# Weight sums of one batch queued in small groups behind dense adds, their tiles fetched a step ahead, and block sums made later

## The chip, the cores and the metric

The kernel runs on one core of a Trainium2 chip. TensorE multiplies matrices, VectorE (DVE in the profile), ScalarE (ACT) and GpSimd (POOL) work element by element, and SyncE (SP) issues nearly all of the transfers between memory and SBUF. The engines run side by side; each works through its own instructions in the order in which the program puts them. The metric is the device time of one execution in microseconds, lower is better, as the median of several runs.

## The reference

An attention block feeds a block that mixes with a Fourier transform. There are 4 batches, 8 heads, 768 tokens and 64 elements per head, all in fp32. Cut to what matters:

```python
# attention: a window of +-15 tokens, and 24 block summaries per head
k_sum = k.reshape(B, H, nb, 32, D).max(axis=3)
v_sum = v.reshape(B, H, nb, 32, D).mean(axis=3)
scores_l = where(|i - j| < 16, q @ k.T / 8, -1e9)
scores_s = q @ k_sum.T / 8 + log(32)
a = softmax(concat([scores_l, scores_s]))
x = a @ concat([v, v_sum])            # heads side by side: (B, 768, 512)
# mixing
u = x + real(fft(fft(x, axis=1), axis=2))
un = (u - mean(u)) / sqrt(var(u) + 1e-6)
out = u + max(un @ w_ch1, 0) @ w_ch2  # 512 -> 2048 -> 512
```

## The kernel before

The four batches go through a pipeline: while batch b is in its two dense layers, the attention of batch b+1 is worked on beside it.

The two dense layers are made with Strassen's scheme in Winograd's form: seven products of half-size blocks in place of eight. That needs sums of the blocks of both operands. `_left_sums` and `_right_sums` make four such sums each (L477 to L488). The first layer is `gen_hidden(b, c)` (L1278): c is the half of the hidden units, and each half has four steps j of 256 units. One step is seven products (L1293, called hx, hy and hz by the accumulator that they go to), with copies, adds and relus on ScalarE and VectorE in between (L1303 to L1322). A product is 1.29 us of TensorE. The second layer is `gen_out(b, c)` (L1326): three groups of rows, each with four sums of the hidden block on VectorE (s, L1348 to L1351), and seven products of four matmuls (ox, oy, oz, L1358), each added to x by VectorE.

The weights come in as fp64 words and are converted once, during batch 0, by `gen_weights` (L1090) on VectorE and ScalarE; the finished tiles with their sums are stored to DRAM and fetched again by the later batches. An exception are the first four tiles of the second layer: batch 0 stores only their blocks without the sums (L1078 to L1080). In batch 1 `get_w2` (L1112) fetches each of these four (called w, w2_1_0 to w2_1_3), makes the four sums on VectorE at once, and stores them for batches 2 and 3. `gen_hidden` calls `get_w2` for tile j at the head of step j (L1285); the tile's user is `gen_out(1, 0)`, after step 3. The tiles live in four buffers that hold the second half's tiles of the batch before until its last products have read them.

Attention works on four pairs of heads g (`gen_attention`, L960): scores (sc, L776), scores of the block summaries (ss, L792), an exponential on ScalarE and a mask product on VectorE (p with near, L783), then values (`values`, L795): a small product with the block sums (vs, L799), its product with a mask on VectorE (L800), the window's values (av, L809), and the block sums' values (av, L814), which read vs. For the next pair VectorE transposes K and Q (L693) and takes the maximum of each block (km, L717).

The block sums of V themselves (`block_sums`, L604) are made for two pairs at a time, (b, 0) and (b, 1): four loads on SP (vb), and adds that run on VectorE while weights are still being converted, and on GpSimd afterwards (L629 to L639). On GpSimd they use the one large buffer called room, which the Fourier stage also uses. `load_values` calls `block_sums` at odd g for the pairs that come after (L652, L653): block (2, 0) during the attention of batch 1, which runs beside batch 0's dense layers, and (3, 0) during the attention of batch 2. Block (b, 1) of the later batches is made at g = 1 of its own attention (L994).

What sets the order: `drive` (L1422) steps several generators in turn by given rates (in one round, 44 steps of the dense layers and 76 of the attention, L1473), which gives the order in which instructions are recorded; a scheduler then orders them on each engine by its own estimates of when operands are ready, except for the first attention, whose order is fixed by hand. `tc.issue_after(marks["dense"])` keeps an instruction behind the last dense add that was marked. The transfers recorded after batch 0 begins its dense layers may be reordered too (L1469).

Of the kernel before, what the change touches and what calls it, by code (L numbers as in the profile page):

```python
# [483 lines left out]
def _right_sums(tt, b):  # L484
    tt(b(T1), b(B12), b(B11), ALU.subtract)
    tt(b(T2), b(B22), b(T1), ALU.subtract)
    tt(b(T3), b(B22), b(B12), ALU.subtract)
    tt(b(T4), b(B21), b(T2), ALU.subtract)  # L488


def _main_program(ctx, tc, q, k, v, moe_w_ch1, moe_w_ch2, out):
# [3 lines left out]
    B, H, S, D = q.shape  # L495
# [69 lines left out]
    def tt(out, in0, in1, op):  # L565
        return nc.vector.tensor_tensor(out=out, in0=in0, in1=in1, op=op).ins  # L566
# [7 lines left out]
    def load(b, g, *which):  # L574

        for n in which or (1, 0):
            t = nat[b, g, n] = apool.tile([P, 2, NST // 2, 2 * D], FP, tag="nat", bufs=4, name=f"{'qk'[n]}n_{b}_{g}")
            if (b, g) > (2, 0):
                t = nat[b, g, n] = t.rearrange("p e j n -> p (e j n)").rearrange("p (m c) -> p m c", c=32)
                for e in range(2):  # L580
                    for h in range(2):
                        r, o = D * e + 32 * h, (q, k)[n][b, 2 * g + e].offset + 32 * h
                        fetch(out=t[r:r + 32], in_=bass.AP((q, k)[n].tensor, o, [[D, 32], [32 * D, S // 32], [1, 32]]))
                continue
            fetch(out=t.rearrange("p e j n -> p (e j) n"),
                  in_=(q, k)[n][b, 2 * g:2 * g + 2].rearrange("e (j p s) d -> p (e j) (s d)", p=P, s=2))
# [61 lines left out]
    def load_values(b, g):  # L648
        if is_wide(b):
            load_wide_values(b, g)  # L650
            return
        if g % 2 and following(b, g, 1) and (b, g) != (1, 1) and not (b > 1 and g == 1):  # L652
            block_sums(*divmod((b * NP + g + 1) // 2, NP // 2))  # L653
        load_narrow_values(b, g)

    def load_wide_values(b, g):
# [169 lines left out]
    def following(b, g, n):  # L826
        i = b * NP + g + n
        return divmod(i, NP) if i < B * NP else None
# [131 lines left out]
    def gen_attention(b):  # L960
        x = bpool.tile([P, NST, DM], FP, tag="x", bufs=2, name=f"x_{b}")
        x_of[b] = x
        held = None
        if b == 2:
            load(2, 1)
            load(2, 2)
        for g in range(NP + 1):
            n1, n3 = (following(b, g, n) for n in (1, 3))
            if held:
                values(b, g - 1, *held, x)  # L970
                if n1 and b > 1:
                    load_values(*n1)
            if g == NP and b > 1:
                turn_tiles(b, x)
                for _ in range(17):
                    yield
                rooms[b] = room(f"fold_{b}")
                steps = fold_batch(b, split_fold(b, rooms[b]))
                while True:
                    with tc.issue_after(marks["dense"]):  # L980
                        done = next(steps, steps) is steps
                    if done:
                        break
                    yield
            elif held and b > 1:
                yield
                yield
                yield
            if g < NP:
                held = scores(b, g)  # L990
                sum_scores(b, g, held[1])
            if g and n1 and b == 1:
                load_values(*n1)
            if g == 1 and b > 1:  # L994
                block_sums(b, 1)
            if g == NP and b > 1:
                return
            yield
            if g == NP:
                return  # L1000
            if b > 1:
                yield
                yield
            if n1:
                prepare(*n1, *((1,) if b > 1 else ()))
            if b > 1:
                yield
                yield
                if n1:
                    prepare(*n1, 0)  # L1010
            if n3 and not (b == 1 and n3 > (2, 0)):
                load(*n3)
            yield
            if b > 1:
                yield
# [89 lines left out]
    def get_w1(b, j):  # L1105
# [3 lines left out]
        fetch(out=w, in_=dw1[j])  # L1109
        wt[1, b, j] = w  # L1110

    def get_w2(b, j):  # L1112
        w = bpool.tile([P, 7, HD], FP, tag="w2", bufs=NC, name=f"w2_{b}_{j}")
        if b == 0:
            return
        wt[2, b, j] = w
        if b == 1 and j < NC:
            fetch(out=w[:, 0:4], in_=dw2[j][:, 0:4])
            _right_sums(tt, lambda i: w[:, i])
            fetch(out=dw2[j][:, 1:7], in_=w[:, 1:7])  # L1120
        else:
            fetch(out=w, in_=dw2[j])

# [154 lines left out]
    def gen_hidden(b, c):  # L1278
        u = wt["u", b]
        js = range(NC * c, NC * (c + 1))  # L1280
        h = wt["h", b] = bpool.tile([P, NC, 2, S], FP, tag="h", name=f"h_{b}_{c}")
        for j in js:
            if 0 < j < NJ - 2:
                get_w1(b, j + 2)
            get_w2(b, j)  # L1285
            w = wt[1, b, j]
            c11, c12 = h[:, j - NC * c, 0, 0:S2], h[:, j - NC * c, 0, S2:S]
            c21, c22 = h[:, j - NC * c, 1, 0:S2], h[:, j - NC * c, 1, S2:S]
            X, Y, Z = (bank([P, S2], f"h{n}_{b}_{j}") for n in "xyz")

            def product(ps, a, r, start, stop):
                for kk in range(2):
                    ins = nc.tensor.matmul(ps, w[:, a, kk, :], u[:, r, kk, :], start=start and kk == 0,  # L1293
                                           stop=stop and kk == 1, skip_group_check=True)
                marks["hidden", b] = ins.ins

            def relu(t):
                if b:
                    nc.vector.tensor_scalar(out=t, in0=t, scalar1=0.0, scalar2=None, op0=ALU.max)
                else:  # L1300
                    nc.scalar.activation(out=t, in_=t, func=AF.Relu)

            product(X, A11, B11, True, False)  # L1303
            nc.scalar.copy(out=c11, in_=X)  # L1304
            product(Y, A12, B21, True, True)
            marks["dense"] = tt(c11, Y, c11, ADD)
            yield
            product(X, S2_, T2, False, False)
            nc.scalar.copy(out=c12, in_=X)
            product(Z, S1, T1, True, False)  # L1310
            nc.scalar.copy(out=c22, in_=Z)  # L1311
            relu(c11)
            yield
            product(X, S3, T3, False, False)
            marks["dense"] = tt(c22, X, c22, ADD)
            product(Z, S4, B22, False, True)
            marks["dense"] = tt(c12, Z, c12, ADD)
            yield
            product(X, A22, T4, False, True)
            nc.scalar.activation(out=c21, in_=X, func=AF.Relu)  # L1320
            relu(c22)
            relu(c12)  # L1322
            issued.add(("h", b, j))
            yield

    def gen_out(b, c):  # L1326
# [137 lines left out]
    for b in range(B):  # L1464


        most = chain(gen_hidden(b, 0), gen_out(b, 0), gen_hidden(b, 1))
        if b == 0:
            in_order[0] = False  # L1469
            drive((most, 5, 0), (weights, 15, 0), (attn, 1, 0))  # L1470
            done_weights.append(True)
        else:
            drive((most, 44, 0), (gen_attention(b + 1) if b + 1 < B else iter(()), 76, 0))  # L1473
        last = gen_out(b, 1)
        if b + 1 < B:
            drive((gen_fourier(b + 1), 22, 600), (last, 12, 0))
        else:
            drive((last, 1, 0))
        if b == B - 2:

            ok = apool.tile([P, B * NP * 2 * NST], FP, tag="qt", name="ok")
            all_ok = spool.tile([P, 2], FP, tag="all_ok", name="all_ok")
            flag = cpool.tile([1, 1], I32, name="flag")
            rv = rec.rearrange("p n h i -> p (n h i)")
            nc.vector.tensor_scalar(out=ok, in0=rv, scalar1=1.0 / LIM, scalar2=None, op0=ALU.is_ge)
            nc.vector.scalar_tensor_tensor(out=ok, in0=rv, scalar=LIM, in1=ok, op0=ALU.is_le, op1=ALU.mult)
            nc.vector.tensor_reduce(out=all_ok[:, 0:1], in_=ok, op=ALU.min, axis=AX.X)
            nc.vector.memset(all_ok[:, 1:2], 1.0)
            ps = bank([1, 1], "flag_ps")
            nc.tensor.matmul(ps, all_ok[:, 0:1], all_ok[:, 1:2], start=True, stop=True)  # L1490
            nc.vector.tensor_scalar(out=flag, in0=ps, scalar1=P - 0.5, scalar2=None, op0=ALU.is_lt)
# [40 lines left out]
```

## Time and profile before

| | us |
|---|---|
| median of 3 runs | 810.48 |
| lowest and highest | 807.29, 811.65 |
| the profiled execution | 811.17 |
| its span, first to last instruction | 809.3 |
| TensorE matmul busy | 781.9 (97%) |
| TensorE weight load busy, beside it | 571.9 (71%) |
| VectorE busy | 500.8 (62%) |
| ScalarE busy | 224.3 (28%) |
| GpSimd busy | 46.8 (6%) |

The stages, by the span's own clock: the first attention until about 60 us; batch 0's first layer with the weights' conversion and the attention of batch 1, about 92 to 149; its second layer and second half until 287; batch 1's first half from there to 388, and its second half with the Fourier stage of batch 2 until 478; batch 2 likewise until 659; batch 3, with no attention beside it, to the end. A busy TensorE is not TensorE at its peak: its ends are modelled. The name before an arrow is the tile written, behind it the tiles read. The profile's numbers for one product are doubled against the program's: each fp32 matmul shows as two records.

### The profile page before, as it was taken

What the parts mean: (1) busy time and instruction counts of PE and PEld (TensorE: products, weight loads), DVE (VectorE), ACT (ScalarE), POOL (GpSimd) and SP (SyncE); (2) the same over time, 40 slices, a digit from 0 to 9 for tenths busy, and PEclk for the clock granted to TensorE, in tenths of its full rate; (3) what the DMA queues carried; (4) which work ended last, traced back from release to release, by engine and by line L of the source; (5) the groups of instructions that cost most, each with busy time, mean ns of one, the idle gap of its engine ahead of it and who ended that gap; (6) DMA issues with size and microseconds to landing.
All of it is one profiled execution on the core that took longest, in us unless ns stands there. A gap on an engine that the chain in (4) does not pass through costs nothing.

```text
span 809.3 us, 14447 instructions
## 1 busy us (share of the span) xinstructions
PE 781.9 (97%) x5914; PEld 571.9 (71%) x5914; DVE 500.8 (62%) x1135; ACT 224.3 (28%) x493; POOL 46.8 (6%) x85
## 2 busy tenths in 40 slices
PE   8959899999999989999999999999999999999997
PEld 6758665555579856678669876688669875786686
DVE  5778998887998664554476734554476722532352
ACT  3523865543635112200126112200126102001200
POOL 0010000000000220010030300000030000000000
PEclk9979999999999999999999999999999999999999
DMA  9999799769655367939344248511514043205001
GB/s 218 222 198 179 162 320 271 155 224 298 214 165 174 93 202 184 206 86 173 117 176 153 66 160 174 156 48 53 227 40 153 37 171 149 87 0 228 0 28 55
DMA packets 135258, 121.83 MB, mean 151 GB/s; under 512 B 94448, under 2 KB 116688, under 8 KB 134992
## 3 DMA queue, kind: packets, MB, share of 16 engines
q1 hardware_dynamic: 133920, 118.53, 53.3%
q0 software_dynamic: 576, 2.10, 0.8%
q8 instruction: 48, 0.79, 0.4%
q10 hardware_dynamic: 688, 0.20, 0.1%
q14 instruction: 26, 0.21, 0.1%
HBM read 97.22 MB, written 23.59 MB: 149 GB/s over the span
## 4 chain that ended last, share of the span: by engine, by line
PE 89%; DVE 5%; ACT 2%; DMA 2%; SPq 1%; issue 1%; POOL 0%; DVEq 0%; ACTq 0%; POOLq 0%
PE hx L1293 20%; PE ox L1358 17%; PE hz L1293 10%; PE oz L1358 9%; PE o L1335 5%; PE hy L1293 5%; PE oy L1358 4%; PE y L1193 3%; PE sc L776 2%; PE mx L1152 2%; PE av L814 1%; PE av L809 1%; PE unt L1271 1%; DVE w L566 1%; SPq L553 1%; PE qk L702 1%
## 5 line engine op out<-in xcount | busy, mean ns | idle before, releaser
L1293 PE MATMUL hx<-u,w 128*128 128x384 f32 x512 | 187.2, 493 | 3.8 <-DVE h L566 3.8
L1293 PEld LDWEIGHTS hx<-u,w 128*128 128x128 f32 x512 | 95.7, 191 | 72.3 <-DVE h L566 5.7
L1293 PE MATMUL hz<-u,w 128*128 128x384 f32 x256 | 93.2, 487 | 0.0
L1358 PE MATMUL oz<-w,s 128*128 128x256 f32 x336 | 81.6, 380 | 0.6 <-DVE w L566 0.6
L1358 PE MATMUL ox<-w,s 128*128 128x256 f32 x336 | 80.3, 380 | 1.3 <-DVE x L566 1.3
L1358 PE MATMUL ox<-w,h 128*128 128x256 f32 x336 | 79.6, 380 | 0.0
L566 DVE TENSOR_TENSOR x<-ox,x 128x256 f32<-128x256 f32 x84 | 35.3, 422 | 69.5 <-PE ox L1358 69.2
L1293 PEld LDWEIGHTS hz<-u,w 128*128 128x128 f32 x256 | 48.5, 190 | 34.0 <-ACT h L1311 0.5
L1358 PEld LDWEIGHTS oz<-w,s 128*128 128x128 f32 x336 | 63.3, 190 | 10.6 <-issue 1.2
L1358 PEld LDWEIGHTS ox<-w,s 128*128 128x128 f32 x336 | 63.1, 190 | 10.7 <-DVE x L566 2.3
L1358 PEld LDWEIGHTS ox<-w,h 128*128 128x128 f32 x336 | 63.2, 190 | 9.6 <-DVE x L566 0.3
L1304 ACT COPY h<-hx 128x384 f32<-128x384 f32 x32 | 15.3, 479 | 169.9 <-PE hx L1293 169.9
L1293 PE MATMUL hy<-u,w 128*128 128x384 f32 x128 | 46.7, 488 | 0.0
L566 DVE TENSOR_TENSOR h<-hx,h 128x384 f32<-128x384 f32 x32 | 17.8, 555 | 46.4 <-PE hx L1293 46.1
L566 DVE TENSOR_TENSOR h<-hy,h 128x384 f32<-128x384 f32 x32 | 17.8, 555 | 45.3 <-PE hy L1293 45.3
L1320 ACT ACTIVATE h<-hx 128x384 f32<-128x384 f32 x32 | 15.7, 491 | 94.5 <-PE hx L1293 94.5
L1335 PE MATMUL o<-w,h 128*128 128x512 f32 x96 | 41.8, 593 | 0.0
L1358 PE MATMUL oy<-w,h 128*128 128x256 f32 x168 | 40.2, 379 | 0.0
L1293 PEld LDWEIGHTS hy<-u,w 128*128 128x128 f32 x128 | 24.1, 190 | 16.3
L566 DVE TENSOR_TENSOR x<-oz,x 128x256 f32<-128x256 f32 x42 | 17.7, 422 | 28.8 <-PE oz L1358 28.5
L1358 PEld LDWEIGHTS oy<-w,h 128*128 128x128 f32 x168 | 31.9, 190 | 4.3
L1335 PEld LDWEIGHTS o<-w,h 128*128 128x128 f32 x96 | 18.1, 190 | 21.9 <-issue 20.6
(164 smaller groups left out, 1099.5 us busy)
## 6 DMA issues: line engine op xcount, KB each, us to landing
w<-dw SPq DMA_DIRECT2D x44, 896.0 KB, 5.6
words<-in_moe_w_ch_dram SPq DMA_DIRECT2D x32, 512.0 KB, 6.6
dw<-w SPq DMA_DIRECT2D x12, 896.0 KB, 6.2
vw<-in_v_dram SPq DMA_DIRECT2D x47, 192.0 KB, 5.2
out_dram<-x SPq DMA_DIRECT2D x24, 256.0 KB, 2.2
vb<-in_v_dram SPq DMA_DIRECT2D x24, 192.0 KB, 4.0
kn<-in_k_dram SPq DMA_DIRECT2D x9, 384.0 KB, 5.4
qn<-in_q_dram SPq DMA_DIRECT2D x9, 384.0 KB, 7.8
```

Source lines behind the costliest of these rows:

```text
L553: ins = nc.sync.dma_start(out=out, in_=in_)
L566: return nc.vector.tensor_tensor(out=out, in0=in0, in1=in1, op=op).ins
L702: nc.tensor.matmul(ps[D * e:D * (e + 1), 2 * P * (j - j0) + s:2 * P * (j - j0 + 1):2], src[:, e, j, D * s:D * (s + 1)], ident, start=True, ...
L776: nc.tensor.matmul(ps[h][r:r + 64, i, :], kt[rows, o:o + 64], qt[rows, o:o + BLOCK], start=True, stop=True)
L809: nc.tensor.matmul(av[r][32 * j:32 * (j + 1), t, :], p[rows, h, i - NB2 * h, :], vw[rows, i, :], start=(t == 0), stop=False, skip_group_ch ...
L1152: nc.tensor.matmul(out, y[:, g], table, start=False, stop=True, skip_group_check=True)
L1193: nc.tensor.matmul(y, fgs[b][par][:, st, P * g:P * (g + 1)], fs[par][:, g % 2, st, :], start=(st == 0), stop=(st == n - 1))
L1293: ins = nc.tensor.matmul(ps, w[:, a, kk, :], u[:, r, kk, :], start=start and kk == 0, stop=stop and kk == 1, skip_group_check=True)
L1304: nc.scalar.copy(out=c11, in_=X)
L1320: nc.scalar.activation(out=c21, in_=X, func=AF.Relu)
L1335: nc.tensor.matmul(ps, h[:, n, hf, P * t:P * (t + 1)], wt[2, b, j][:, 2 * hf:2 * hf + 2, :], start=(n, hf) == (0, 0), stop=(n, hf) == (NC ...
L1358: nc.tensor.matmul(ps, left[a][:, n, :], wt[2, b, j][:, r, :], start=start and n == 0, stop=stop and n == NC - 1, skip_group_check=True)
```

## The change

In batch 1's first half the tiles of the second layer are fetched a step ahead: tiles 0 and 1 at step 0, tile 2 at step 1, tile 3 at step 2. Their sums and stores aren't issued at the fetch; they are put on a list, `to_sum`. From step 1 on, at each of the four places where `gen_hidden` yields, `some_sums(3)` issues the next three of the list behind the last marked dense add. The list holds 4 tiles x (4 sums + 1 store) = 20 entries.

`block_sums(b, 0)` for b = 2 and 3 is called no longer in `load_values` but at the start of `gen_attention(b)`, which then lets four steps pass before its first scores. The attention's rate goes from 76 to 80 for the four steps more.

```diff
@@ load_values
-        if g % 2 and following(b, g, 1) and (b, g) != (1, 1) and not (b > 1 and g == 1):
-            block_sums(*divmod((b * NP + g + 1) // 2, NP // 2))
         load_narrow_values(b, g)
@@ gen_attention
         if b == 2:
             load(2, 1)
             load(2, 2)
+        if b > 1:
+            block_sums(b, 0)
+            for _ in range(4):
+                yield
         for g in range(NP + 1):
@@ before get_w2
+    to_sum = []
+
+    def some_sums(n):
+        with tc.issue_after(marks["dense"]):
+            for f, a in to_sum[:n]:
+                f(*a)
+        del to_sum[:n]
+
@@ get_w2
         if b == 1 and j < NC:
             fetch(out=w[:, 0:4], in_=dw2[j][:, 0:4])
-            _right_sums(tt, lambda i: w[:, i])
-            fetch(out=dw2[j][:, 1:7], in_=w[:, 1:7])
+            _right_sums(lambda *a: to_sum.append((tt, a)), lambda i: w[:, i])
+            to_sum.append((fetch, (dw2[j][:, 1:7], w[:, 1:7])))
@@ gen_hidden
-            get_w2(b, j)
+            if (b, c) != (1, 0):
+                get_w2(b, j)
+            else:
+                for i in ((0, 1), (2,), (3,), ())[j]:
+                    get_w2(b, i)
...
             marks["dense"] = tt(c11, Y, c11, ADD)
+            some_sums(3 if (b, c) == (1, 0) and j else 0)
             yield
...
             relu(c11)
+            some_sums(3 if (b, c) == (1, 0) and j else 0)
             yield
...
             marks["dense"] = tt(c12, Z, c12, ADD)
+            some_sums(3 if (b, c) == (1, 0) and j else 0)
             yield
...
             issued.add(("h", b, j))
+            some_sums(3 if (b, c) == (1, 0) and j else 0)
             yield
@@ the rounds
-            drive((most, 44, 0), (gen_attention(b + 1) if b + 1 < B else iter(()), 76, 0))
+            drive((most, 44, 0), (gen_attention(b + 1) if b + 1 < B else iter(()), 80, 0))
```

## The prediction

> **What bounds the kernel now.** I read the busy table, then TensorE's waits, then the timeline around the longest, then sums over two stages that do the same work.
>
> ```profile
> PE 781.9 (97%) x5914; PEld 571.9 (71%) x5914; DVE 500.8 (62%) x1135; ACT 224.3 (28%) x493; POOL 46.8 (6%) x85
> PEclk9979999999999999999999999999999999999999
> ```
>
> ```profile
> PE hx L1293 <- DVE h L566: 3.8, 1, 3.8
> ...
> PE oz L1358 <- DVE w L566: 0.6, 1, 0.6
> ...
> PE sc L776 <- ACT qt L712: 1.0, 1, 1.0
> ```
>
> TensorE sets the end; only some 27 us of the span are free of it, 11 of them in the first 60 us. The second fence lists TensorE's waits (us in total, times, longest); those the change can reach are few. The timeline (start, length, engine, line, tiles) shows how the longest arises, at the start of batch 1's first layer:
>
> ```profile
> 285.77 0.43 SPq L553 DMA_DIRECT2D w<-dw  x1
> ...
> 292.00 1.95 DVE L566 TENSOR_TENSOR w<-w 128x256 f32<-128x256 f32 x2 [4.55 <-DMA w<-dw]
> ...
> 296.61 0.54 DVE L566 TENSOR_TENSOR h<-hy,h 128x384 f32<-128x384 f32 x1
> ...
> 301.00 2.93 PE L1293 MATMUL hx<-u,w 128*128 128x384 f32 x4 [3.77 <-DVE h L566]
> ```
>
> VectorE stands at the first weight sum until the tile has landed; the dense add of hy, whose product TensorE ended at about 291.6, comes only at 296.6, and TensorE then has no accumulator to go on with. In stretches of 2 us (TensorE busy, weight loads, VectorE, ScalarE, GpSimd, granted clock):
>
> ```profile
> 297.00:299.00 2.00, 0.23 (x1) 0.00 (x0) 2.00 (x4) 0.00 (x0) 0.00 (x0) 1.00 0.94 366
> 299.00:301.00 2.00, 0.00 (x1) 0.00 (x1) 2.00 (x7) 0.00 (x0) 0.00 (x0) 0.80 0.96 169
> 301.00:303.00 2.00, 2.00 (x3) 1.17 (x4) 2.00 (x5) 0.00 (x0) 0.00 (x0) 0.50 0.35 56
> 303.00:305.00 2.00, 2.00 (x64) 1.50 (x67) 1.09 (x4) 0.49 (x1) 0.00 (x0) 0.50 0.34 56
> 305.00:307.00 2.00, 2.00 (x69) 1.83 (x56) 0.00 (x0) 0.00 (x0) 0.00 (x0) 0.50 0.94 155
> ```
>
> The wait costs twice: 3.77 us idle, and then 6 us at half clock, so about 3 us more. What the whole stage loses is read from a control inside the same run. From the last product of the old batch to the first product of the layer's second half, batches 1 and 2 issue the same TensorE work, but only batch 1 makes weight sums:
>
> ```profile
> 286.99:387.99 101.00, 96.28 (x1137) 70.39 (x1138) 53.46 (x113) 12.84 (x28) 8.60 (x10) 0.97 0.80 171
> 477.73:570.28 92.55, 92.19 (x1138) 68.26 (x1138) 45.05 (x97) 12.91 (x28) 1.78 (x2) 1.00 0.45 123
> ```
>
> The difference is 8.45 us: 3.77 idle, 3.0 clock, 0.62 + 0.33 at 356.9 and 358.4 where the fourth tile's sums are late, and restarts.
>
> [...]3.77 us idle, then 0.50 for about 6 us; waits of 0.3 to 1.0 us left the clock at 1.00. [...]one weight sum at 292.57, with GpSimd busy beside it, took 1.37 us, against a median of 0.416.
>
> **The change part by part**, on the order in which the built programs' instructions stand on each engine.
>
> (a) Weight sums of batch 1: 4 tiles x 4 sums, and 4 stores. No operation is added or removed. They stood ahead of the stage's first dense add; now hy_0, the relus, both mask products, hx_0, hz_0, a transpose, the reduction and hy_1 precede the first. By then (some 14 us after the stage begins) the tile has long landed: its load cannot issue before about 285.8 (it waits for the last readers of its buffer), and took 6.1 us. So the wait goes, and the half clock with it. The 16 sums take 16 x 0.41 = 6.6 us of VectorE, which batch 2's stage shows 45.05 us busy of 92.55; that idle time is the cover. The tightest place is the first head pair's value sums: between hy_1 and the product with vs stand hy's add 0.48, a transpose 0.89, six short sums and a relu, together about 3.7 us, against 3.9 us of TensorE work (two products at 1.29, vs 0.17, values 1.13): no charge; if the cover failed, 0.5 us. The load of the fourth tile moves from behind j=2 to directly behind the third, and its sums end before j=3, so the two late waits go too. The stage should run at batch 2's pace: -8.45 us.
>
> (b) Attention starts four steps later, so four of the seven products of j=0 come ahead of the scores, and for the third head pair both products ox and oy come ahead of vs and the values. On VectorE the product with vs now stands behind hz_3's add, a transpose 0.89, relu 0.26, reduction 0.94, a second transpose 0.89, four left sums at 0.60 to 0.67 and two adds at 0.34: from hz_3's end about 6.9 us until vs is written. TensorE has one more hx 1.29, ox 1.73, oy 1.73, vs 0.17 and the values 1.13, 6.05 us. The next products need vs: a new wait of about 0.85 us, in batch 1 and in batch 2. Bounds: 0 (the values took 1.58 us where they were slow[...]) to 2.5 each. 2 x 0.85 = +1.7.[...] In batch 1 the fourth pair's values are also cut up between products; the control's are not: two more switches at 0.2 (1.49 against 1.29 after each): +0.4.
>
> (c) Block sums (2,0) leave batch 0's stage: 3 adds at 0.68 and a reduction at 1.0, 3.05 us of VectorE, and 4 loads on SP. They become GpSimd's in batch 1's turn: three adds at 1.26, two smaller ones and a last of 0.32, about 6.2 us as for the block at 277.8 to 284.0. Their room comes free with the last transposes (268.7), so they are ready at about 282; the reader comes after 300. Block (2,1) follows where (3,0) stood; (3,0) moves to batch 2's turn, where GpSimd is idle. On SP, the loads of block (2,1) end before 285.8, as those of (3,0) did. Cost nothing.
>
> In batch 0's stage VectorE is nearly full. Dropping the sums, the order of TensorE changes: the ten products of j=1 to j=3 stand in one piece ahead of the fourth pair's scores, which before were cut in four and waited for ScalarE:
>
> ```profile
> 128.70 1.00 PE sc L776 x26
> 129.70 1.49 PE hx L1293 x4
> 131.19 0.81 PE sc L776 x22
> ...
> 136.26 0.69 PE sc L776 x18
> ...
> 145.76 1.04 PE sc L776 x30
> ```
>
> Before, 127.68 to 149.07 is 21.4 us. In one piece: 11 products x 1.29 = 14.2, scores 1.53, sum scores 0.78, values 0.87 and five switches x 0.2 = 18.4: 3.0 us less, if VectorE keeps up. Bounds 0 to -3.0, as the weights for the second layer are made just in time there, and the last tile is stored at 228.3 for a reader at about 231.6. VectorE's own 3.05 us less cover most of this. I take -2.0.
>
> (d) Loads and stores on SP shift: the fourth w1 tile comes ahead of the K and Q loads and then waits for j=0's end (about 298); K and Q of pair 3 follow, needed some 40 us later; stores of the sums wait for the sums, with loads behind them that have 15 us or more. Nothing. The fold of the next batch keeps its place near the stage's end: turned tiles about 10 us later, still some 10 us ahead of their reader. Nothing.
>
> Sum: -8.45 + 1.7 + 0.4 - 2.0 = -8.35. The profiled execution took 811.17 us (span 809.3), so 802.8; on the median of 810.48, 802.1.
>
> **Rivals.**
> 1. The weight sums' wait is traded for the vs wait at its upper bound in both batches, and batch 0's stage gives nothing: -8.45 + 0.4 + 5.0 = -3.05, 807.4. For: [...]with eight more instructions ahead of vs. Against: four of them are 0.3 to 0.6 us.
> 2. The change does not do what it says: the sums still meet a tile that has not landed, or the stores hold up the loads; 810.5. The instruction order speaks against it.
> 3. [...]The place is the end of the third pair's stage; each wait of w costs w + 3.0 at half clock. That outweighs the gain from w = 1.0 on[...]; at w = 4, 2 x 7.0 - 8.45 + 0.4 = +5.95, 816.4. Against: it needs VectorE to be 3 us later than the listed durations make it.
>
> **How the numbers follow.** Main case 0.80; rival 1 0.10; rival 2 0.03; rival 3 0.07. A measurement of this kernel can tell about 0.5%, 4 us: faster is below 806.4, slower above 814.5. So faster 0.80, same 0.13, slower 0.07. The range: best, no vs wait and the whole 3.0 in batch 0, 810.48 - 8.45 + 0.4 - 3.0 = 799.4, and a little below it for the run-to-run spread of 807.3 to 811.7; worst, rival 1 at 807.4. 798.8 to 807.4.
>
> **What would show it.** (a) right: no wait of hx on h at batch 1's start, clock 1.00 all through, a stage of about 94 us. (b) right: a wait of values (L814 before) on VectorE's vs of near 1 us in batches 1 and 2. (c) right: the second layer of batch 0 starts at 146 to 149, and GpSimd adds a block near 275. Wrong: a clock below 1.00 after 290, or batch 2's stage longer than 95 us.

## The result

| | before | changed |
|---|---|---|
| median of 10 runs each, us | 809.82 | 802.83 |
| lowest and highest | 807.11, 814.75 | 799.68, 805.90 |
| profiled execution and its span | 811.17, 809.3 | 800.91, 799.1 |

The ratio is 0.9914, with a 95% interval of 0.9886 to 0.9943: 7.0 us faster, between 4.6 and 9.2. The forecast was 8.35.

Two lines of the page of the changed kernel: its busy table, and the granted clock over the span.

```profile
PE 775.9 (97%) x5914; PEld 566.1 (71%) x5914; DVE 496.6 (62%) x1131; ACT 224.5 (28%) x493; POOL 52.0 (7%) x91
...
PEclk8999999999999999999999999999999999999999
```

TensorE's waits over the whole span (total us, times, longest):

```profile
PE av L812 <- DVE vs L566: 1.5, 2, 0.7
...
PE ox L1376 <- DVE x L566: 0.9, 1, 0.9
...
PE sc L774 <- issue: 0.5, 1, 0.5
...
PE hx L1307 <- DVE h L566: 0.3, 1, 0.3
```

The wait of hx on h of 3.8 us at batch 1's start is gone (the 0.3 in the list lies in batch 0's first layer), and the new wait of the values on vs has come, 0.72 us in batch 1 and 0.75 in batch 2. The timeline of the changed kernel shows the start of batch 1's layer as forecast: the first dense add at once, the first weight sum 12 us later.

```profile
283.09 10.96 SPq L553 DMA_DIRECT2D w<-dw  x4
...
284.86 0.56 DVE L566 TENSOR_TENSOR h<-hy,h 128x384 f32<-128x384 f32 x1 [2.23 <-PE hy L1307]
...
296.87 0.41 DVE L566 TENSOR_TENSOR w<-w 128x256 f32<-128x256 f32 x1
```

Busy sums over three stages of the changed kernel: batch 0's first layer, batch 1's first half, batch 2's first half.

```profile
89.30:144.06 54.76, 52.82 (x579) 32.01 (x573) 51.84 (x108) 37.83 (x75) 0.00 (x0) 1.00 0.82 233
282.17:377.59 95.42, 94.15 (x1137) 68.84 (x1137) 52.08 (x113) 12.87 (x28) 4.31 (x8) 1.00 0.76 172
467.33:560.05 92.72, 91.97 (x1138) 67.80 (x1137) 45.04 (x97) 12.83 (x28) 1.78 (x2) 1.00 0.48 123
```

Before, the last two took 101.00 and 92.55. So batch 1 gains 5.58 of the 7.2 forecast for it (8.45 - 0.85 - 0.4), and batch 2 loses 0.17. From the first product of batch 0's first layer to the first of its second layer, 56.85 us have become 54.69 (the window above ends 0.07 us later). The rest is equal within 0.2 us, except the start: the first dense product comes at 92.06 before and at 89.30 here, but in the twelve other profiles below that share the code up to that point it falls anywhere from 90.8 to 95.0. Those 2.76 us belong to the two profiled executions and not to the change; stages are therefore compared here by their own length.

TensorE is short of batch 2's pace by 2.7 us in batch 1. The largest part lies where the fourth head pair's values (av) stand between the second layer's products:

```profile
359.36 0.33 PE L797 MATMUL vs<-vbs,sel 96*128 96x64 f32 x2
359.62 0.55 PE L807 MATMUL av<-vw,p 64*32 64x65 f32 x24
360.10 1.56 PE L1376 MATMUL ox<-w,h 128*128 128x256 f32 x6
361.59 0.88 PE L807 MATMUL av<-vw,p 64*32 64x65 f32 x48
362.40 0.93 PE L812 MATMUL av<-vs,p 64*128 64x130 f32 x6
363.27 1.13 PE L1376 MATMUL ox<-w,h 128*128 128x256 f32 x4
364.33 0.55 PE L807 MATMUL av<-vw,p 64*32 64x65 f32 x24
364.80 0.93 PE L812 MATMUL av<-vs,p 64*128 64x130 f32 x6
365.67 1.56 PE L1376 MATMUL ox<-w,h 128*128 128x256 f32 x6
367.06 1.89 PE L1376 MATMUL oy<-w,h 128*128 128x256 f32 x8
```

From 359.36 to 367.06 are 7.70 us, with no wait in them. In the kernel group2 below the same products, with the values in one stretch, take 6.57. It is the switching that costs, 1.13 us at this place.

### The profile page after: what moved, and what is told of

It reads as the page before. It is cut to its first block, busy times and chain, and to the rows that moved or that the text cites. A ratio compares the mean times of both kernels' runs of the same rounds, so it can differ in the third digit from the quotient of the medians.

```text
span 799.1 us, 14452 instructions
## 1 busy us (share of the span) xinstructions
PE 775.9 (97%) x5914; PEld 566.1 (71%) x5914; DVE 496.6 (62%) x1131; ACT 224.5 (28%) x493; POOL 52.0 (7%) x91
## 4 chain that ended last, share of the span: by engine, by line
PE 84%; DVE 12%; DMA 2%; issue 1%; ACT 1%; ACTq 0%; SPq 0%; DVEq 0%
PE hx L1307 19%; PE ox L1376 17%; PE hz L1307 9%; PE oz L1376 9%; PE o L1353 5%; PE hy L1307 5%; PE oy L1376 4%; PE y L1203 3%; PE mx L1162 2%; PE sc L774 2%; DVE x L566 2%; DMA half<-c_half 1%; PE av L812 1%; PE av L807 1%; DVE u L566 1%; DVE w L566 1%
```

## The experiments

Theory A is the prediction's: the weight sums' place in VectorE's queue made the stall. The rivals as they came up: B, the later start of the attention is what helps; C, batch 0's block sums bring it all; D, the earlier fetch does; and, after the second set, E: block (3, 0), whose loads and GpSimd adds fell on the stage's start in the kernel before, made the tile late and VectorE slow.

The change has four parts: the list of sums, the fetch a step ahead, the delay of four steps, and the moved block sums. Batch 1's stage is measured from the last product of the old batch to the last of its first half, as before. Batch 0 is from its first dense product to the first of its second layer. Ratios are to the kernel before as it was measured beside each kernel; its medians there were 809.82 to 811.16.

| kernel | list | ahead | delay | moved | batch 0 | batch 1 | median | ratio (95%) |
|---|---|---|---|---|---|---|---|---|
| before | | | | | 56.85 | 101.00 | | |
| changed | x | x | x | x | 54.69 | 95.42 | 802.83 | 0.9914 (0.9886 to 0.9943) |
| sums_only | x | x | | | 56.81 | 91.88 | 803.28 | 0.9906 (0.9875 to 0.9938) |
| no_lead | x | x | | x | 54.70 | 91.88 | 800.05 | 0.9875 (0.9845 to 0.9906) |
| list_moved | x | | | x | 54.67 | 91.89 | 800.97 | 0.9879 (0.9845 to 0.9912) |
| no_ahead | x | | x | x | 54.70 | 93.43 | 801.70 | 0.9910 (0.9879 to 0.9940) |
| group2 | x | x | x | x | 55.15 | 93.88 | 801.73 | 0.9893 (0.9865 to 0.9922) |
| sums_at_fetch | | x | x | x | 54.69 | 94.62 | 802.23 | 0.9894 (0.9861 to 0.9926) |
| fetch_only | | x | | x | 54.68 | 94.51 | 802.30 | 0.9916 (0.9884 to 0.9947) |
| blocks_only | | | x | x | 54.69 | 95.67 | 804.22 | 0.9922 (0.9894 to 0.9951) |
| moved_only | | | | x | 54.68 | 95.60 | 803.94 | 0.9917 (0.9888 to 0.9945) |

The times alone do not separate kernels that lie within some 3 us of each other; the stages do. Each stage is read from one profile, though: group2's batch 0 has the code and the order of products of the changed kernel, and took 0.46 us longer. Three further kernels (ahead2, no_adds, no_block) are told of below.

### The list with the fetch ahead, and without the delay

sums_only is the kernel before with the list and the fetch ahead, shown against the changed kernel:

```diff
-        if b > 1:
-            block_sums(b, 0)
-            for _ in range(4):
-                yield
...
+        if g % 2 and following(b, g, 1) and (b, g) != (1, 1) and not (b > 1 and g == 1):
+            block_sums(*divmod((b * NP + g + 1) // 2, NP // 2))
...
-iter(()), 80, 0)
+iter(()), 76, 0)
```

> The kernel before with the weight sums' list and the fetch ahead alone: the block sums and the attention's start stay as before. Theory A[...]: no wait of hx on VectorE's h at batch 1's start, clock 1.00 there, batch 1's stage 92.9 us (batch 2's 92.55 plus a little for the sums), batch 2's stage 92.5, batch 0's first layer as before at 57.0; about -8.1 us, 801.7. Rival B (the gain comes from the attention that starts four steps later, dense products ahead of the scores): the stage stays at 98 us or more, 807 or more. Rival C (the change's gain is nearly all one of batch 0's block sums): no gain, 809.

no_lead is the changed kernel without the delay:

```diff
             block_sums(b, 0)
-            for _ in range(4):
-                yield
...
-iter(()), 80, 0)
+iter(()), 76, 0)
```

> The changed kernel without the four steps ahead of the attention, rate 76: sums on the list and block sums moved. Theory A: batch 1's stage 92.9 us, batch 2's 92.5 and no wait of the values on VectorE's vs (0.72 and 0.75 us in the changed kernel), the fourth pair's values in one piece; batch 0's first layer 54.8 us. About -10.3 against the kernel before, 799.5, so some 2.5 to 3 us faster than the changed kernel. If the block sums' move gives nothing in batch 0, equal to the kernel with the sums alone; if it gives what the profile shows, 2.2 us less than that one. Rival B: slower than the changed kernel by 3 us or more.

Busy sums over batch 1's stage of sums_only (us; TensorE, weight loads, VectorE, ScalarE, GpSimd; clock, DMA share, GB/s):

```profile
286.70:378.58 91.88, 91.88 (x1138) 68.06 (x1138) 51.62 (x113) 12.83 (x28) 8.03 (x10) 1.00 0.84 188
```

TensorE is busy for the whole stage. List and fetch ahead together take 9.12 us off it, more than the 8.45 that the control of batch 2 promised, and GpSimd's 8.03 us with block (3, 0) still in the stage cost TensorE nothing. The list without the fetch ahead was run only with the block sums moved (list_moved). B and C fall. no_lead repeats the 91.88 and adds 2.1 us in batch 0: the move of block (2, 0) off VectorE. Against them the changed kernel loses 3.54 us in batch 1, by its delay; without the fetch ahead the delay costs 1.54 (no_ahead against list_moved). In batch 2 the delay costs next to nothing (92.66 without, 92.72 with it): there the kernels without it have an idle gap in the fourth pair's scores, shown with ahead2 below, and that gap is in the control of the kernel before too (0.4 us), which was therefore slower than it could be.

### The cut-up values

group2 lets two entries of the list pass at each place in place of three; nothing else of TensorE's order changes but that pair 4's values stand in one stretch.

```diff
-            some_sums(3 if (b, c) == (1, 0) and j else 0)
+            some_sums(2 if (b, c) == (1, 0) and j else 0)
```

> The changed kernel with two entries of the list at each place in place of three: TensorE's order differs only in that batch 1's fourth pair's values stand in one piece. Theory A, with the cut-up values at 1.85 us: batch 1's stage 93.6 us in place of 95.4, all else as in the changed kernel, 801.0. If the cut costs what I forecast for it, 0.4 us: 95.0, 802.4. If VectorE's sums spread over more places are late for the second layer: a wait of oz on w, stage above 95.4.

The same place in the timeline of group2:

```profile
361.28 0.33 PE L797 MATMUL vs<-vbs,sel 96*128 96x64 f32 x2
361.54 1.07 PE L807 MATMUL av<-vw,p 64*32 64x65 f32 x72
362.54 0.49 PE L812 MATMUL av<-vs,p 64*128 64x130 f32 x2
362.95 0.55 PE L807 MATMUL av<-vw,p 64*32 64x65 f32 x24
363.43 0.93 PE L812 MATMUL av<-vs,p 64*128 64x130 f32 x10
364.29 3.72 PE L1376 MATMUL ox<-w,h 128*128 128x256 f32 x16
367.85 1.89 PE L1376 MATMUL oy<-w,h 128*128 128x256 f32 x8
```

And of no_lead:

```profile
356.52 0.33 PE L797 MATMUL vs<-vbs,sel 96*128 96x64 f32 x2
356.78 1.20 PE L807 MATMUL av<-vw,p 64*32 64x65 f32 x96
357.91 0.94 PE L812 MATMUL av<-vs,p 64*128 64x130 f32 x12
358.78 1.99 PE L1374 MATMUL ox<-w,s 128*128 128x256 f32 x8
```

group2's stage is 1.54 us shorter, as theory A had it. That contains an idle gap of 0.55 us that only the changed kernel has, and a further wait on vs of 0.39 that only group2 has; TensorE's busy time, free of both, falls from 94.15 to 92.77, by 1.38, and the place itself by 1.13 (7.70 to 6.57). Even the change between the two forms of value products costs: vs and all values take 2.26 us in no_lead, where the forms stand apart, and 3.01 in group2, where they alternate once more.

### Which part cures the stall

sums_at_fetch keeps all but the list:

```diff
-            _right_sums(lambda *a: to_sum.append((tt, a)), lambda i: w[:, i])
-            to_sum.append((fetch, (dw2[j][:, 1:7], w[:, 1:7])))
+            _right_sums(tt, lambda i: w[:, i])
+            fetch(out=dw2[j][:, 1:7], in_=w[:, 1:7])
```

> The changed kernel with the fetch ahead kept, but the sums and stores issued at the fetch, with no list: the sums of tile 0 stand ahead of the first dense add, those of tiles 1 and 2 ahead of the second. Theory A: the stall is back, hx on VectorE's h 3.8 us or more, clock 0.50 after it, batch 1's stage 100 to 106 us; near or above the kernel before less the 2.2 us of batch 0, 807 to 813. Rival D (fetching the tiles earlier is what helps): stage at 95 us, 803.

Here theory A missed. The sums stand in front of the dense adds again, but the timeline of sums_at_fetch shows a short stall:

```profile
286.55 1.55 DVE L566 TENSOR_TENSOR w<-w 128x256 f32<-128x256 f32 x4 [2.43 <-DMA w<-dw]
...
288.02 0.55 DVE L566 TENSOR_TENSOR h<-hy,h 128x384 f32<-128x384 f32 x1
...
291.45 2.69 DVE L566 TENSOR_TENSOR w<-w 128x256 f32<-128x256 f32 x7 [2.49 <-DMA w<-dw]
...
295.94 2.85 PE L1307 MATMUL hx<-u,w 128*128 128x384 f32 x8 [2.03 <-DVE h L566]
```

The first tile's load issued at 282.39, as long before the old batch's last product as it had in the kernel before (1.27 us against 1.21), but it served the first sum after 4.16 us in place of 6.23. Something else had delayed it. Three kernels asked what: fetch_only (this one without the delay), blocks_only (the kernel before with the move and the delay) and moved_only (the kernel before with the move alone).

```diff
@@ fetch_only, against sums_at_fetch
-            for _ in range(4):
-                yield
...
-iter(()), 80, 0)
+iter(()), 76, 0)
@@ moved_only, against fetch_only
-            if (b, c) != (1, 0):
-                get_w2(b, j)
-            else:
-                for i in ((0, 1), (2,), (3,), ())[j]:
-                    get_w2(b, i)
+            get_w2(b, j)
```

> Block sums moved and the tiles fetched a step ahead, but the sums issued at the fetch and the attention not delayed: on VectorE one piece and six weight sums stand ahead of hy's and hx's first adds, as before. Stages to compare with: batch 1's took 101.0 us before, 91.7 with the list and no delay, 94.5 with delay and fetch ahead but no list. Theory A (the sums' place costs; an earlier fetch does not cure it): [...]stage 98 to 102, 806 to 810. Rival D (the earlier fetch cures it): stage under 94, 801 to 802.

> The kernel before with the block sums moved and the attention four steps later, and nothing done to the weight sums: on VectorE 4 sums stand ahead of the first dense add and 8 more, of tiles 1 and 2, ahead of the second. Theory A with the delay as a partial cover (four products ahead of the scores run during the wait, so the stall of 2.0 us seen with the fetch ahead grows only by what tile 2's later fetch adds): stall of 2 to 5 us; stage 95 to 101 us. Rival B (the delay alone is what cures batch 1): stage at 95 or less, 802 or 803, no more than the changed kernel.[...]

> The kernel before with the block sums moved and nothing else: VectorE's order at batch 1's start is that of the kernel before, with one piece and six weight sums ahead of the first dense adds. Theory A (the sums' place alone makes the stall): stall of hx on h 3.8 us, half clock after it, batch 1's stage near 101, only batch 0's 2.2 us gained, 808. Theory E (in the kernel before, block (3, 0)'s loads and GpSimd adds fall on the stage's first 8 us, make the tile late and VectorE slow; with them away the same order does not stall for long): stall 1 to 1.5 us, clock 1.00, stage 94 to 96, 802 to 804.

The stall was 0.97 us in fetch_only, 1.02 in blocks_only and 0.95 in moved_only, with the clock at 1.00 in all. The last has VectorE's order of the kernel before at this place, unchanged. Its timeline (issue of the tile's load; first weight sums; masks; first product that waits):

```profile
284.78 0.34 SPq L553 DMA_DIRECT2D w<-dw  x1
...
289.27 0.89 DVE L566 TENSOR_TENSOR w<-w 128x256 f32<-128x256 f32 x2 [2.77 <-DMA w<-dw]
...
290.08 1.02 DVE L566 TENSOR_TENSOR p<-p,near 128x384 f32<-128x384 f32 x2
...
297.25 1.56 PE L1301 MATMUL hx<-u,w 128*128 128x384 f32 x4 [0.95 <-DVE h L566]
...
350.57 0.70 PE L1370 MATMUL oz<-w,s 128*128 128x256 f32 x2 [0.62 <-DVE w L566]
```

In the kernel before, block (3, 0) stood at this place. The last four of these five loads are its own, just ahead of the tile's load at 285.77, and GpSimd's adds run beside VectorE's first weight sums and masks:

```profile
276.66 9.07 SPq L553 DMA_DIRECT2D vb<-in_v_dram  x5
...
290.99 4.27 POOL L569 TENSOR_TENSOR vb<-vb 96x512 f32<-96x512 f32 x4 [2.31 <-DMA vb<-in_v_dram]
...
293.87 1.81 DVE L566 TENSOR_TENSOR p<-p,near 128x384 f32<-128x384 f32 x2
```

With the blocks moved the tile serves after 4.49 us, two sums take 0.89 (1.95 before), two masks 1.02 (1.81 before). Theory E holds: the moved blocks alone take 5.4 us from the stage. Neither the fetch ahead nor the delay is needed for that. The long stalls that theory A gave (2 to 5 us in blocks_only, 3.8 in moved_only) were missed, and so were its stage of 98 us or more in fetch_only, D's of under 94 and B's of 95 or less.

The fetch ahead is worth something of its own here. Where the sums are made at the fetch, it takes 1.1 us more from the stage: 94.51 against 95.60 without the delay, 94.62 against 95.67 with it. The two late waits of the second layer, 0.62 and 0.33 us, are still there in moved_only and blocks_only and gone in fetch_only and sums_at_fetch. The list takes the same waits away.

### Loads or adds

no_adds is the kernel before without all but the last add of block (3, 0); no_block leaves out three of its four loads too.

```diff
+        if (b, gg) == (3, 0):
+            gtt(vb, raw[0][:, 0:D], raw[0][:, D:2 * D], ADD)
+            return
@@ no_block, besides
-        for i in range(4):
+        for i in range(1 if (b, gg) == (3, 0) else 4):
             fetch(out=raw[i], in_=src[:, n * i:n * (i + 1)])
```

> The kernel before with the GpSimd adds of block (3, 0) left out but for the last small one; its four loads stay. What is left out is the sum over a block's values that batch 3's first two head pairs read, so its time is that of a kernel without these adds. The order on TensorE, VectorE and SP is unchanged. Theory E[...]: the first weight sums and mask products at 0.45 and 0.5 us each in place of 0.98 and 0.9, the stall shorter by 1.5 to 2 us, so 2 us and no half clock: stage 96 to 97. Theory E with the loads as the cause: the tile still lands 6 us after its issue[...], stage 100 to 101. Theory A: 100 to 101.

> As the kernel without block (3, 0)'s adds, with three of its four loads left out too, so that the same sum of batch 3 is missing. Theory E with the loads as a cause: the first tile lands 4 to 4.5 us after its issue in place of 6.2, on top of what the adds give; stall under 1 us, stage 93 to 95. If the loads do not matter: equal to the kernel without the adds alone. Theory A: still 100 to 101.

The timeline of no_adds:

```profile
287.20 0.43 SPq L553 DMA_DIRECT2D w<-dw  x1
...
293.41 0.89 DVE L566 TENSOR_TENSOR w<-w 128x256 f32<-128x256 f32 x2 [4.94 <-DMA w<-dw]
...
301.56 2.86 PE L1296 MATMUL hx<-u,w 128*128 128x384 f32 x4 [3.30 <-DVE h L566]
```

Its windows (us busy of TensorE, weight loads, VectorE, ScalarE, GpSimd; clock):

```profile
301.00:303.00 2.00, 1.45 (x3) 0.84 (x4) 2.00 (x7) 0.00 (x0) 0.00 (x0) 0.66 0.63 100
303.00:305.00 2.00, 2.00 (x30) 1.28 (x36) 1.25 (x4) 0.49 (x1) 0.00 (x0) 0.50 0.07 12
305.00:307.00 2.00, 2.00 (x106) 1.78 (x87) 0.50 (x3) 0.00 (x0) 0.00 (x0) 0.98 0.97 157
...
288.01:387.56 99.55, 95.30 (x1137) 69.50 (x1138) 51.70 (x113) 12.82 (x28) 3.28 (x5) 0.98 0.81 174
```

The timeline of no_block:

```profile
284.88 0.34 SPq L553 DMA_DIRECT2D w<-dw  x1
...
289.29 0.88 DVE L566 TENSOR_TENSOR w<-w 128x256 f32<-128x256 f32 x2 [2.68 <-DMA w<-dw]
...
297.46 1.56 PE L1296 MATMUL hx<-u,w 128*128 128x384 f32 x4 [1.07 <-DVE h L566]
```

With the adds gone VectorE is fast (0.89), but the tile is as late as before (6.21 us), and behind the stall of 3.30 us the clock is at 0.50: the stage is 99.55. Leaving out the adds was worth 1.45 us: 0.47 of idle time, and 0.98 of TensorE's busy time, since the half clock lasted about 3.4 us (by the clock of the first three stretches) in place of 6.83. The forecast for the adds as the cause, 96 to 97, missed. Median 809.01, ratio 0.9981 (0.9957 to 1.0004). With three of the four loads gone as well the tile serves after 4.41 us, the stall is 1.07, and the stage is 95.73: 3.8 us more, and within 0.13 of moved_only. Median 806.24, ratio 0.9939 (0.9921 to 0.9956). The four loads are of 192 KB each. What leaving out the loads with the adds kept would give was not run, so the two shares hold for this order only.

### The fetch ahead

no_ahead drops it from the changed kernel, list_moved from the kernel without the delay too; ahead2 gives it to batch 2 as well.

```diff
@@ ahead2, against no_lead
-            if (b, c) != (1, 0):
+            if (b, c) not in ((1, 0), (2, 0)):
                 get_w2(b, j)
```

> The changed kernel with the list and the delay, but each tile fetched in its own step as before: TensorE's order is that of the changed kernel with batch 1's fourth pair's values in one piece. If the fetch ahead is not needed for the gain: batch 1's stage 93.7 us as with two entries at each place, 801 to 802. If the fetch ahead carries a part: the fourth tile's sums are late for the second layer, waits of oz on w of 0.5 to 1 us as before, stage 94.5 or more.

> The changed kernel with neither the attention's delay nor the fetch ahead: the list of sums and the moved block sums alone. TensorE's order is that of the kernel without the delay. If the fetch ahead carries nothing, batch 1's stage is 91.9 us as there, batch 2's 92.6, batch 0's first layer 54.9, and the time 799 to 801. If the fetch ahead is needed once the delay is gone: sums late for the second layer, waits of oz on w of 0.6 us or more, stage 92.5 to 94, 801 to 802.

> The changed kernel without the attention's delay, and with the second layer's tiles fetched a step ahead in batch 2 as in batch 1. Without the delay batch 2's stage took 92.50 us against 91.72 of batch 1: its first products of the second layer were cut in two (the fourth tile taken to be late) with an idle gap of 0.42 us. If the later fetch is the cause, the order becomes batch 1's and the stage 91.7 us: 0.8 us less than without, 799.2, the fastest so far. If the fetch ahead collides with the loads of K and Q: a wait on a transpose, and no gain.

no_ahead's stage is 2.0 us shorter than the changed kernel's, and list_moved's is 91.89: beside the list the fetch ahead carries nothing in batch 1. With groups of three and the delay it is what leads to the cut-up values; no_lead, which has it without the delay, keeps them in one piece.

ahead2 put batch 2's second-layer products in one piece as planned, and its stage went from 92.66 only to 92.57; the forecast of 0.8 missed. What stayed is an idle gap in the scores, for which the profile names no releaser. The scores take 2.27 us here in place of 1.60, and those 0.67 us are nearly all of the 0.69 that batch 2 has over batch 1 (91.88):

```profile
520.56 1.01 PE L774 MATMUL sc<-qt,kt 64*64 64x32 f32 x55
522.04 0.79 PE L774 MATMUL sc<-qt,kt 64*64 64x32 f32 x41 [0.47 <-issue]
```

With 799.24 us, ratio 0.9876 (0.9846 to 0.9907), it is the lowest median of all, level with no_lead and list_moved. Their intervals overlap the changed kernel's; that they are faster than it rests on the 3.5 us of batch 1's stage. The smallest edit of the three is list_moved.

## Why the prediction came out as it did

**What bounds the kernel.** Right as far as it went: TensorE, with the stall at batch 1's start as what could be had. The stretch of 8.45 us against batch 2 was a good control for size, though itself some 0.7 us above the 91.88 that the stage can reach.

**(a) Weight sums.** Right in sign, place and size for what list and fetch ahead do: 9.12 measured, 8.45 forecast. VectorE's idle time covers the sums, and no dense add waits for them. But the reason was half of one. I read the wait for the tile and the queue behind it, and did not ask why the tile took 6.2 us: block (3, 0)'s loads, ahead of it on SP, and GpSimd's adds beside VectorE's first sums. That VectorE passed the delay on shows in the kernel before:

```profile
288.55 0.87 ACT L782 ACTIVATE p<-sc 128x384 f32<-128x384 f32 x2 [20.13 <-PE sc L776]
...
293.87 1.81 DVE L566 TENSOR_TENSOR p<-p,near 128x384 f32<-128x384 f32 x2
```

ScalarE had written p by 289.42, and VectorE stood idle until 292.00, but the mask products of p came only at 293.87, behind the two sums. So the sums' place in the order was needed for the stall and not sufficient: with the same order on VectorE, moved_only waits 0.95 us.

**(b) Delay.** The new wait is there at 0.72 and 0.75 us, forecast 0.85 each, and the clock stayed at 1.00 over both stages. The term that was mis-sized is the cut-up values: I took two more switches at 0.2 us, +0.4. The profile shows the values in three stretches, so four more switches with products between, and the two forms of value product alternate besides. Of the 3.54 us that the delay costs in batch 1 beside list and fetch ahead, 1.27 is idle: the wait on vs, 0.72, and a gap in the second pair's scores, 0.55, whose cause stays open (the same label stands in batch 2 of kernels without the delay). 2.27 is TensorE busy for longer (94.15 against 91.88): 1.38 by the cut, by group2, and 0.89 that group2 still has, of which the alternating forms are 0.75 (3.01 against 2.26). In place of 0.85 + 0.4 stand 0.72 + 0.55 + 2.27.

**(c) Block sums.** Batch 0: -2.0 forecast, -2.1 by sums_only against no_lead. "Cost nothing" for the move of block (3, 0) out of batch 1's turn was the wrong step in kind: moving it is worth 5.4 us by itself. The prediction had noted that its loads end just ahead of the tile's, and did not ask what that did to the tile. The 5.4 us did not show in the sum, since the list removes the same stall; the two do not add up (5.4 for the blocks alone, 9.1 for list and fetch ahead alone, 9.1 for all three).

**(d)** Right: no wait of TensorE on a load after the start appeared.

**The sum.** -5.58 in batch 1, -2.16 in batch 0 and +0.17 in batch 2 make -7.6; the medians say -7.0 and the prediction said -8.35. That the total came so near is partly luck. In batch 1 the delay cost 2.3 us more than forecast (3.54 for 0.85 + 0.4). Against that the list gave 0.7 more, and batch 2 lost 0.7 less, because a gap of 0.4 us in its scores, which the prediction had not reckoned with, went away as the new wait came. Rivals 1 and 3 needed a vs wait of 2.5 and 4 us in each of the two batches; it was never above 0.75. Rival 2 is ruled out by the vanished stall.

## What to carry to other kernels

When a wait ends on a transfer, look at what was issued ahead of that transfer and what runs beside it before crediting the queue that passes the delay on; there may be two cures, and they don't add up. Try the parts of a change singly and beside each other: here one part (the delay) gave back 3.5 of 9.1 us, and another (the fetch ahead) was worth 1.1 us without the list, nothing beside it, and cost 2.0 beside list and delay. Count in the new instruction order how often small products are cut up between large ones, and price every switch.

## What was not expected of the hardware

- When a GpSimd add starts decides what it costs here. In the stage before batch 1's, VectorE makes three sums of u. Where GpSimd's first block add began 1.85 to 2.3 us after the first of them, as in the changed kernel and six others, the three took 2.68 or 2.69 us; in the changed kernel the third had begun at 1.7, and GpSimd's add took 1.96 us, in place of the 1.26 of such an add in the kernel before (at 277.77). Where it began 1.56 to 1.68 us after, ahead of the third, the sums took 3.76, the add in moved_only 1.32, and TensorE waited 1.01 us. That is fetch_only, blocks_only and moved_only, whose stage before, the second half's part of batch 0's second layer, took 57.9 us in place of 56.8 (not in the table's batch 1). What the two engines wait for in each other the traces don't show. That moving block (2, 0) cost nothing, as (c) had it, thus hangs on some 0.2 us. Timeline of fetch_only:

```profile
271.52 3.76 DVE L566 TENSOR_TENSOR u<-u 128x768 f32<-128x768 f32 x3
273.20 6.54 POOL L569 TENSOR_TENSOR vb<-vb 96x512 f32<-96x512 f32 x5 [41.07 <-DMA vb<-in_v_dram]
275.67 2.86 PE L1374 MATMUL ox<-w,h 128*128 128x256 f32 x12 [1.01 <-DVE x L566]
```

- Behind a wait of 3.30 us the clock fell to half (no_adds), as it did behind the one of 3.77 in the kernel before; behind one of 2.03 (sums_at_fetch) it did not. But near 81 us it could fall behind a shorter one. There twelve of the profiles, both kernels' among them, have a wait of TensorE of 1.80 or 1.81 us ahead of vs, with short products and small gaps behind it. In the kernel before the wait ended at 82.42, and the clock was at 0.50 from 85.18 to 88.59. In the changed kernel it ended at 80.66, and the clock stayed at 1.00. In the 3.41 us up to the fall TensorE had been busy for 2.03 us; in the same stretch of the changed kernel (80.01 to 83.42) it was busy for 2.03 as well. The eleven records of unt that follow took 1.42 us in the changed kernel, group2, moved_only and no_block, and 2.17 to 2.61 in the other eight, the kernel before (2.27) among them. What decides between the two was not shown. From 92 us up to the last 3 us, where TensorE has ended, the traces of the two kernels show one fall: that behind the 3.77 us. Over batch 1's first half the granted clock was 0.97 in the kernel before, 0.98 in no_adds, and 1.00 in the twelve others. The half clock lasted 6.8 us behind the wait of 3.77 (300.22 to 307.05), about 3.4 behind that of 3.30, and 3.41 near 85 us in the kernel before.
